# Query projections in column tiles, a written-out order of all operations, keys by another queue and a halved last group in an attention and squared-ReLU kernel

## The chip, the cores and the metric

The kernel runs on one core of one Trainium2 chip. The metric is the device time of one execution in microseconds (us), and less is better. Five engines work side by side and meet through semaphores: TensorE (PE, matmuls), VectorE (DVE), ScalarE (ACT), GpSimd (POOL) and SyncE (SP, which here only issues DMAs). Each engine takes its own instructions strictly in the order in which they were written for it. A wait of one instruction therefore holds up all that stand behind it on the same engine.

## What is computed

Two stages follow each other. The first is attention with a polynomial sketch of degree 2: every query and key row of 32 values is projected by S1 and S2 to 8 + 8 values, and the 64 products of these are its features. The second is a feed-forward layer with a squared ReLU.

```python
# q, k, v: (4 batches, 4 heads, 1088 tokens, 32); S1, S2: (8, 32)
a, b = x @ S1.T, x @ S2.T                 # per token 8 and 8
phi(x) = (a[..., :, None] * b[..., None, :])       # 64 features
kv  = sum over tokens of phi(k)^T v       # 64 x 32 per batch and head
z   = sum over tokens of phi(k)
num, den = phi(q) @ kv, phi(q) @ z + 1e-6
x   = num / den                           # heads side by side: (4352, 128)
h   = x @ w_in                            # w_in (128, 2048)
out = relu(h) ** 2 @ w_out                # w_out (2048, 128)
```

## The kernel before

**Tiling.** The 4352 tokens are handled in chunks of columns: 0a and 0b (256 tokens each), 1 to 7 (512 each) and 8 (the 4 x 64 tokens left over, 256). For each chunk the feed-forward part (`f_stage`) runs 16 column tiles of w_in in groups. A group is F1 (two matmuls with 512 columns, or four with 256, into one of two double PSUM banks "h"), then relu on ACT, then the square "sq" over two groups at a time on DVE (four of them on ACT), then F2 (the product with w_out, four matmuls with 512 columns or sixteen with 128, summed in the one PSUM bank "o"). At the end of a chunk "osb" takes the bank to SBUF and SP stores it.

**Attention of a batch**, which has to come before its two chunks. Keys (`k_stage`): a DVE transpose kT, eight matmuls K1 in four column tiles of 32, a DVE transpose kab back to token-major, the 64-fold products kp on POOL, the sums z and kv on PE, and transposes of the result (KV4T). Queries (`token_major`): for each 512 tokens, qpr multiplies four blocks of 128 query columns, as the stationary operand, with the 96 columns of Wt (S1, S2, and S2 weighted by z). That is a full 128 x 128 weight load for each block. ACT copies the first factor out of PSUM (qa). DVE then forms the denominator (ac, den, rec), divides (a'), makes the 64 products per head (qo, with one operand still in PSUM) and turns them in blocks of 32 x 32 (qd, `turned`). `x_turned` multiplies with KV4 in 32 x 32 tiles, and the results xT are cast to bf16 as input of F1.

**Order.** All operations are recorded with their operands (`Plan.op`, about 530 of them) and laid out by a list scheduler (`Plan.run`): each time it takes, of the operations that can start soonest on an engine, the one with the earliest due time. Due times (`deadlines`) come from a pace of the chunks (STEP), leads, and a table of hand-set shifts (NUDGE). Ahead of the first F1 small matmuls on a constant (line 901) fill the gaps that the plan leaves on PE.

**Loads.** Batch 0: keys in two parts, queries in two (q0.0 with 8 columns and q0.1 with 26), and values, by SP; the last two of the 34 key columns (k0.r) by POOL. POOL then waits for q0.0 (gate) and issues w_in, two products kp of batch 0, the keys of batch 1, w_out, and everything else.

Of the kernel before, what the change touches and what calls it, by code (L numbers as in the profile page):

```python
# [12 lines left out]
ALU = mybir.AluOpType  # L13
# [4 lines left out]
class Op:  # L18
    __slots__ = ("eng", "fn", "name", "preds", "succs", "dma", "base", "dl", "allocs", "uses", "n", "start", "end", "lead", "pri", "port")
# [6 lines left out]
HOP, DELTA, FIX, TAIL, AHEAD = 0.08, 0.06, 1.4, 0.6, 10.4  # L26
FRAC = 0.64
# [4 lines left out]
class Plan:  # L32

# [12 lines left out]
    def op(self, eng, dur, fn, reads=(), writes=(), name="", dma=None, base=None, lead=0.0, pri=None, port=False):  # L46
        o = Op()
        o.eng = [(eng, dur + 0.13 if eng == "PE" else dur)] if isinstance(eng, str) else list(eng)
        o.fn, o.name, o.dma, o.base, o.lead, o.pri, o.port = fn, name, dma, base, lead, pri, port
# [15 lines left out]
        o.succs, o.n, o.start = [], len(self.ops), None  # L65
        for p in o.preds:
            p.succs.append(o)
# [3 lines left out]
    def deadlines(self, stretch):  # L71
        for o in reversed(self.ops):
            d = 1e9 if o.base is None else o.base
            for s in o.succs:
                d = min(d, s.dl - s.lead)
            o.dl = d - (min(x[1] for x in o.eng) * stretch + HOP if o.succs and (o.base is None or d < o.base) else 0)
            if o.dma is not None and o.succs:
                o.dl -= FIX + TAIL + o.dma
        done = set()
        for name, early in (("xT0.0", 40.0), ("xT0.1", 10.0)):  # L80
            urgent = {o for o in self.ops if o.name == name}
            for o in reversed(self.ops):
                if o in urgent:
                    urgent.update(o.preds)
                    o.dl -= early if o not in done else 0.0
            done |= urgent
        for o in self.ops:
            o.dl += NUDGE.get(o.name, 0.0)
            if o.pri is not None:
                o.dl = o.pri  # L90

    def run(self, slots, stretch=1.3, t0=0.7):
        self.deadlines(stretch)
# [5 lines left out]

        def places(t):  # L100
            return pool["r"] + pool["t"] if t.kind == "r" else pool["t"]

# [4 lines left out]
        left = {o: len(o.preds) for o in self.ops}  # L107
        ready = {o for o in self.ops if not o.preds}
        order = []
        while ready:  # L110
            best = {}
            for o in sorted(ready, key=lambda o: o.n):
                slot = 0.0
                if o.allocs:
                    at = sorted(places(o.allocs[0]))
                    if len(at) < len(o.allocs):
                        continue
                    slot = at[len(o.allocs) - 1][0] + HOP
                pick = None
                for e, d in o.eng:  # L120
                    s = max(free[e], slot, port if o.port and e in ("DVE", "POOL") else 0.0)
                    if o.dma is not None:
                        l = lane["SW" if e == "POOL" else "HW"]
                        s = max(s, l[-8] if len(l) > 7 else 0.0)
                    for p in o.preds:
                        s = max(s, p.end + (HOP if p.eng[0][0] != e or p.dma is not None else 0.03))
                    if pick is None or s + d < pick[0] + pick[2]:
                        pick = (s, e, d)
                best.setdefault(pick[1], []).append((pick[0], o, pick[2]))
            if not best:  # L130
                raise RuntimeError("no operation can go on: " + ", ".join(o.name for o in ready))
            chosen = None
            for e, c in sorted(best.items()):
                m = min(x[0] for x in c) + DELTA
                s, o, d = min((x for x in c if x[0] <= m), key=lambda x: (x[1].dl, x[1].n))
                for x in sorted(c, key=lambda x: (x[1].dl, x[1].n)):
                    if x[1].dl < o.dl - AHEAD and x[0] < s + FRAC * d:
                        s, o, d = x
                        break
                if chosen is None or s < chosen[0]:  # L140
                    chosen = (s, o, e, d)
            s, o, e, d = chosen
# [4 lines left out]
            if o.dma is not None:  # L147
                q_, x_ = ("SW", "HW") if e == "POOL" else ("HW", "SW")
                begin = max(dmat.get(q_, 0.0), o.end + (1.0 if o.pri is not None else FIX))
                shared = min(max(dmat.get(x_, 0.0) - begin, 0.0), 2 * o.dma) / 2  # L150
                dmat[q_] = begin + o.dma + shared
                dmat[x_] = dmat.get(x_, 0.0) + shared
                o.end = dmat[q_] + TAIL
                lane[q_].append(o.end)
            for t in o.allocs:
                x = min(places(t))
                t.kind, t.i = x[1]
                pool[t.kind].remove(x)
# [5 lines left out]
            order.append(o)  # L164
            ready.discard(o)
            for x in o.succs:
                left[x] -= 1
                if left[x] == 0:
                    ready.add(x)
        assert len(order) == len(self.ops), "operations left over"  # L170
        self.order = sorted(order, key=lambda o: (o.start, o.n))
# [3 lines left out]
STRETCH, BASE0, STEP = 1.27, 19.5, 6.71  # L175
# [4 lines left out]
HOOK = {"1": ("0b", 2), "e1": ("1", 4), "e2": ("3", 4), "e3": ("5", 4), "8": ("6", 4)}  # L180
# [3 lines left out]
NUDGE = {  # L184
    "kp0.6": 15.9, "KV0": -10.1, "qpr0.0": -8.4, "x0.0": -5.2, "den0.1": 12.3, "osb0a": -5.4, "F1 0b.1": 0.1,
    "kabr1": -26.7, "ld vin_0.0": 2.0, "xTe1.B0": 11.2, "F1 1.4": 0.6, "osb2": -2.2, "kp2.0": 18.4, "rec2.1": -7.9,
    "qd2.1": 1.1, "relu 3.5": -0.4, "F2 3.2": -7.7, "osb3": -22.1, "sq 4.0": 2.1, "relu 4.7": 3.5, "kT3": 2.6,
    "kp3.6": 4.8, "qpr3.0": 1.3, "relu 5.6": -1.9, "st o5.11": -19.0, "F2 7.1": 11.4, "relu 7.4": 3.6, "sq 7.3": -14.0,
    "st o7.1": -2.4, "sq 8.0": -8.0,
}  # L190
LEAD = [1.7, 8.8, -7.6, 5.2, 2.4, 1.5, 7.8, 8.9, 2.8]
# [3 lines left out]
def kernel(  # L195
# [33 lines left out]
    S12 = T("S12", [2 * r, H, D])  # L229
# [31 lines left out]
    qaq = ring("qaq", 2, [128, 16, r])  # L261
    t9 = ring("t9", 2, [128, 16, r + 1])
# [26 lines left out]
    def copy(name, eng, o, i, reads, writes, lead=0.0):  # L289
        n = 1  # L290
        for x in o().shape[1:]:
            n *= x
        e = [("ACT", ACT(n)), ("DVE", DVE(n))] if eng == "any" else [(eng, (ACT if eng == "ACT" else DVE)(n))]
        op(e, 0, lambda en: act.copy(o(), i()) if en == "ACT" else dve.tensor_copy(o(), i()),  # L294
           reads, writes, name, lead=lead)
# [44 lines left out]
    for i, x in enumerate((S1, S2)):  # L340
        load("ACT", f"ld S{i}", S12[r * i : r * i + r], x[:, None, :].to_broadcast([r, H, D]), 4, [f"S12.{i}"], first=True)
# [3 lines left out]
    load("POOL", "ld k0.r", K0[:, 32:], rows(k, 0)[:, 32:], 40, [f"{K0k}.r"], first=True)  # L345
# [3 lines left out]
    load("SP", "ld q0.1", Q0[:, 8:], rows(q, 0)[:, 8:], 16.4 * (NJ - 8), [f"{Q0k}.1", f"{Q0k}.2"], first=True)  # L349
# [10 lines left out]
    for i in range(2):  # L360
# [12 lines left out]
    op("PE", 0.17, lambda e: pe.transpose(  # L373
        pb(tp)[:, : 2 * r], S12.rearrange("r h d -> r (h d)"), ident[: 2 * r, : 2 * r]),
# [194 lines left out]
    def token_major(nm, parts, G, X, Xk, xs, kind="t", lead=0.0):  # L569
# [54 lines left out]
        copy(f"xT{nm}", "any", lambda: X, lambda: pb(tx)[:, : 128 * G], [tx], [Xk], lead=lead)  # L624

    def first_part(X, Xk):
# [36 lines left out]
        op("PE", 0.25, lambda e: [pe.matmul(pb(t2)[:, 32 * g : 32 * g + 32], qt[:, 128 * g : 128 * g + 128], Wt[0][:, 2], start=True, stop=True)  # L663
# [12 lines left out]
    def token_chunk(b, nm, c0, G, X, Xk, srcs, kind="t", lead=0.0):  # L676
        qt, qtk = qT(b)
        parts = [(g, 0, qt[:, c0 + 128 * g : c0 + 128 * g + 128], b) for g in range(G)]
        token_major(nm, parts, G, X, Xk, ([(b, slice(0, 128 * G), None)], [(0, 0, f"{qtk}.{x}") for x in srcs]), kind, lead)
# [9 lines left out]
    def x_turned(nm, G, b, qks, outs, lead):  # L689
# [21 lines left out]
        copy(f"xT{nm}.A", "any", lambda: outs[0], lambda: hb[hh][:, :, :n], [f"h{hh}"], [keys[0] + ".0"], lead=lead)  # L711
        for u in range(2):
            copy(f"xT{nm}.B{u}", "any", lambda u=u: outs[1 + u], lambda u=u: pb(ts[u])[:, :n],
                 [ts[u]], [f"{keys[1]}.{u + 1}"], lead=lead)
# [3 lines left out]
    def turned_chunks(nm, b, us, outs, lead):  # L718

        qt, qtk = qT(b)  # L720
        keys = []
# [4 lines left out]
        hooks[HOOK[nm]] = lambda: x_turned(nm, 4 * len(us), b, keys, outs, lead)  # L726

    def token_rest():
# [6 lines left out]
            [Xv[:, 0::2], Xv[:, 1], Xv[:, 3]], (Xk, Xk)), LEAD[8])  # L735
# [6 lines left out]
    def f_stage(nm, X, Xks, N, t0, k, store):  # L742
# [193 lines left out]
```

## Time and profile before

| what | us |
| --- | --- |
| runs shown | 115.51, 120.93, 121.09 |
| median of them | 120.93 |
| the profiled execution: its time | 114.64 |
| its span (first to last instruction) | 112.9 |
| PE, DVE, ACT, POOL busy | 104.6, 89.3, 85.7, 34.0 |
| granted TensorE clock | 1.00 |
| first F1 starts / last F2 ends | 16.68 / 108.81 |

Times on the page are counted from the first instruction. A timeline row gives start, duration, engine, source line, tiles, shapes and how many instructions were merged; in brackets is the idle time before it and what ended that. Matmuls are pipelined, so what one costs PE is read from the start of one group to the start of the next, and not from the duration.

### The profile page before, as it was taken

Reading aid. Unit: us, or ns where it says so; the run is one execution under the profiler, and the core shown is the slowest. Engines: PE = TensorE matmul, PEld = TensorE weight load, DVE = VectorE, ACT = ScalarE, POOL = GpSimd, SP = SyncE. Lnnn points to the kernel's source line nnn. Section 1 sums busy time; section 2 is a strip of 40 time slices with the busy share of each in tenths; the row PEclk is TensorE's granted clock in tenths of the full one; section 3 lists DMA queues with packets and bytes.
Section 4 is the critical chain, followed back from the end, with each engine's and each line's share of the span. In section 5 each row is a group of like instructions: output and inputs, shape, how many; then the busy total and the mean of one; then the engine's idle time right before and its main releaser. Section 6 shows DMA issues by size and latency. Waiting matters only on the chain.

```text
span 112.9 us, 3392 instructions
## 1 busy us (share of the span) xinstructions
PE 104.6 (93%) x1409; PEld 69.6 (62%) x1409; DVE 89.3 (79%) x144; ACT 85.7 (76%) x113; POOL 34.0 (30%) x51
## 2 busy tenths in 40 slices
PE   7999999999999799999999999998999998899750
PEld 5586776688756667874545559445555554479630
DVE  2487569998979997999988999899999837675620
ACT  4342239999999888998558989879689889998920
POOL 7369812499334591000019950000000000000000
PEclk9999999999999999999999999999999999999999
DMA  2989999921887100001100320032004113022022
GB/s 52 322 227 152 305 289 265 333 84 49 227 308 209 49 6 3 0 6 56 36 6 0 58 35 6 0 59 34 6 0 70 23 29 67 3 47 47 6 68 75
DMA packets 16495, 10.20 MB, mean 90 GB/s; under 512 B 11552, under 2 KB 14928, under 8 KB 16480
## 3 DMA queue, kind: packets, MB, share of 16 engines
q0 software_dynamic: 1856, 6.15, 19.7%
q1 hardware_dynamic: 14320, 3.64, 14.3%
q8 instruction: 11, 0.18, 0.7%
q10 hardware_dynamic: 304, 0.20, 0.6%
q14 instruction: 4, 0.03, 0.1%
HBM read 8.81 MB, written 2.23 MB: 98 GB/s over the span
## 4 chain that ended last, share of the span: by engine, by line
PE 65%; DVE 15%; issue 6%; ACT 6%; DMA 3%; POOL 1%; ACTq 0%; POOLq 0%
PE h L765 20%; PE o_ps L789 13%; PE o_ps L792 9%; PE t L581 5%; ACT r L773 5%; DVE qd L684 5%; PE h L705 4%; DMA kin<-in_k_dram 3%; DVE qo L602 3%; PE t L467 3%; PE t L705 2%; PE h L467 1%; PE o_ps L901 1%; DVE g L782 1%; PE t L405 1%
## 5 line engine op out<-in xcount | busy, mean ns | idle before, releaser
L773 ACT ACTIVATE r<-h 128x1024 bf16<-128x1024 f32 x68 | 66.5, 1026 | 6.3 <-PE h L765 5.5
L782 DVE TENSOR_TENSOR g<-r 128x2048 bf16<-128x2048 bf16 x29 | 37.8, 1307 | 7.4 <-ACT r L773 7.2
L765 PE MATMUL h<-xT,w_in 128*128 128x512 bf16 (+1 forms) x128 | 34.9, 373 | 1.1 <-ACT r L773 1.1
L765 PEld LDWEIGHTS <-w_in 128*128 128x128 bf16 x160 | 19.5, 147 | 10.1 <-issue 4.2
L529 POOL TENSOR_TENSOR kp<-kab 128x512 f32<-128x512 f32 x12 | 14.4, 1221 | 21.8 <-DVE kab L509 18.8
L789 PE MATMUL o_ps<-g,w_out 128*128 128x512 bf16 x80 | 20.6, 379 | 0.0
L792 PE MATMUL o_ps<-w_out,g 128*128 128x128 bf16 x224 | 14.8, 219 | 1.5 <-ACT osb L294 0.8
L792 PEld LDWEIGHTS <-g 128*128 128x128 bf16 x224 | 13.3, 98 | 3.5 <-DVE g L782 1.9
L789 PEld LDWEIGHTS <-w_out 128*128 128x128 bf16 x80 | 7.6, 97 | 8.1 <-issue 0.2
L602 DVE TENSOR_TENSOR qo<-qaq,t 128x1024 f32<-128x1024 f32 (+1 forms) x9 | 9.7, 1097 | 0.1
L301 POOL DMA_DIRECT2D vin<-in_v_dram x14 | 7.8, 569 | 4.5 <-PE t L467 3.5
L684 DVE STREAM_TRANSPOSE qd<-qo 128x1024 f32<-128x1024 f32 (+1 forms) x8 | 9.1, 1154 | 0.0
L581 PEld LDWEIGHTS t<-Wt,qT 128*128 128x128 f32 x60 | 7.5, 191 | 0.9 <-issue 0.4
L581 PE MATMUL t<-Wt,qT 128*128 128x96 f32 x60 | 8.0, 277 | 0.0
L782 ACT ACTIVATE g<-r 128x2048 bf16<-128x2048 bf16 x4 | 7.5, 1907 | 0.0
L901 PE MATMUL o_ps<-const-bfloat16-1.0 128*128 128x256 bf16 x33 | 6.4, 338 | 0.8 <-PEq L920 0.8
L467 PEld LDWEIGHTS t<-kp,vin 128*32 128x32 f32 (+1 forms) x216 | 3.7, 108 | 4.7 <-issue 4.5
L705 PE MATMUL h<-qd,KV 32*32 32x256 f32 (+2 forms) x160 | 6.1, 331 | 0.3 <-DVE qd L684 0.3
L705 PE MATMUL t<-qd,KV 32*32 32x256 f32 (+2 forms) x160 | 6.3, 332 | 0.0
L467 PE MATMUL t<-kp,vin 128*32 128x64 f32 (+1 forms) x216 | 6.1, 225 | 0.0
L901 PEld LDWEIGHTS <-const-bfloat16-1.0 128*128 128x128 bf16 x33 | 3.9, 123 | 1.9 <-issue 0.7
L765 PE MATMUL h<-x,w_in 128*128 128x256 bf16 x32 | 4.9, 282 | 0.0
(105 smaller groups left out, 104.2 us busy)
## 6 DMA issues: line engine op xcount, KB each, us to landing
kin<-in_k_dram POOLq DMA_DIRECT2D x3, 544.0 KB, 5.8
qin<-in_q_dram POOLq DMA_DIRECT2D x3, 544.0 KB, 8.7
out_dram<-osb SPq DMA_DIRECT2D x40, 32.0 KB
vin<-in_v_dram POOLq DMA_DIRECT2D x6, 144.0 KB, 5.3
out_dram<-osb SPq DMA_DIRECT2D x13, 64.0 KB
vin<-in_v_dram POOLq DMA_DIRECT2D x6, 128.0 KB, 2.9
kin<-in_k_dram SPq DMA_DIRECT2D x2, 256.0 KB
w_in<-in_moe_w_in_dram POOLq DMA_DIRECT2D x1, 512.0 KB, 5.3
```

The source lines that it names most:

```text
L467: pe.matmul(pb(tv)[32 * h : 32 * h + 32, :64], V[:Pn, h, m, :], kp_[:Pn, m, h].rearrange("p i j -> p (i j)"), start=(m == 0), stop=(m == 8 ...
L529: (pool if e == "POOL" else dve).tensor_tensor(out=kp_[:, 2 * u : 2 * u + 2].rearrange("p m h i j -> p (m h) i j"), in0=x, in1=y, op=ALU.mult)
L581: pe.matmul(o[p0 : p0 + w, :, g], lhs, Wt[b], start=True, stop=True)
L602: dve.tensor_tensor(out=qo_[:, y : y + dy].rearrange("p g h i j -> p (g h) i j"), in0=x_, in1=y_, op=ALU.mult)
L684: op("DVE", DVT(256 * G), lambda e: dve.transpose(qd_[:, g0 : g0 + G].rearrange("p g f t -> p (g f t)"), qo_[:, :G].rearrange("p g h x y - ...
L705: pe.matmul(bank[32 * h : 32 * h + 32, :n], KV4[rg if b is None else b][rows, y, 32 * h : 32 * h + 32], qd_[rows, :G, 2 * h + y, :], start ...
L765: pe.matmul(hv[:, x], w_inv[:, ct], X, start=True, stop=True)
L773: op("ACT", ACT(1024), lambda e, hv=hv, Rv=Rv, own=own: act.activation(Rv[:, own], hv, ACTF.Relu), [f"h{hh}"], [f"{Rk}.{u}"], f"relu {nm}. ...
L782: lambda e, R=R, G=G: dve.tensor_mul(G, R, R) if e == "DVE" else act.activation(G, R, ACTF.Square),
L789: pe.matmul(ob[:, :N], w_out[:, ct], Gv[:, y], start=(ct == 0), stop=(ct == CT - 1), skip_group_check=True)
L792: pe.matmul(ob[:, 128 * tt : 128 * tt + 128], Gv[:, y, tt * 128 : tt * 128 + 128], w_out[:, ct], start=(ct == 0 and tt == 0), stop=(ct == ...
L901: pe.matmul(ob[:, :256], one.to_broadcast([128, 128]), one.to_broadcast([128, 256]), start=True, stop=True)
```

## The change

1. **Queries.** For batches 1 to 3 a new function `compact` takes the place of two calls of `token_major`. The 32 columns of Wt are the stationary operand, and the 1024 query columns move past them in four column tiles: qpr (eight matmuls, both factors) and qpc (four, for the denominator). The results are feature-major, and DVE turns them token-major (qab, 512 elements a partition; qc, 256). The ACT copy qa goes. ac, den, rec and a' are done once for 1024 tokens, and all operands of ac and qo now lie in SBUF.
2. **Order.** `deadlines`, NUDGE and the list scheduler go. `ORDER` lists all operations by number, and `ALT` names 19 that run on the second of two engines given. K1 and kT of later batches, the keys' loads and the stores stand at other places; the hooks that place x_turned move (from group 4 to 6 of the chunk before, for instance).
3. **Loads.** k0.r goes to SP's queue, behind the two other parts of the keys. The rest of the queries is loaded in two parts. S1 and S2 are loaded once and not four times over, and four small matmuls into four column tiles replace their transpose. On POOL the keys of batch 1 are issued ahead of w_in.
4. **Last group** (8.3): relu, sq and F2 each in two halves (named 8.30 and 8.31 on ACT and DVE, 8.1.10 and 8.1.11 on PE).
5. **Stores** of chunks 0a and 1 in halves of 64 rows.

```diff
-LEAD = [1.7, 8.8, ...]  NUDGE = {...}  STRETCH, BASE0, STEP = 1.27, 19.5, 6.71
-HOOK = {"1": ("0b", 2), "e1": ("1", 4), "e2": ("3", 4), "e3": ("5", 4), "8": ("6", 4)}
+HOOK = {"1": ("0b", 3), "e1": ("1", 6), "e2": ("3", 6), "e3": ("5", 6), "8": ("6", 6)}
+HALVES = ("0a", "1")
+ORDER = [0, 3, 16, 1, 4, 17, ...]
+ALT = {116: 1, 127: 1, ...}
...
-    load("POOL", "ld k0.r", K0[:, 32:], rows(k, 0)[:, 32:], 40, [f"{K0k}.r"], first=True)
+    load("SP", "ld k0.r", K0[:, 32:], rows(k, 0)[:, 32:], 40, [f"{K0k}.r"], first=True)
-    load("SP", "ld q0.1", Q0[:, 8:], rows(q, 0)[:, 8:], 16.4 * (NJ - 8), [f"{Q0k}.1", f"{Q0k}.2"], first=True)
+    for key, j0, j1 in (("1", 8, 16), ("2", 16, NJ)):
+        load("SP", f"ld q0.{key}", Q0[:, j0:j1], rows(q, 0)[:, j0:j1], 16.4 * (j1 - j0), [f"{Q0k}.{key}"], first=True)
...
+    def compact(nm, b):
+        qv = qt.rearrange("p (g c t) -> p c g t", c=4, t=32)
+        def mm(e, t, fs):
+            for k_, f in enumerate(fs):
+                for c in range(4):
+                    pe.matmul(pb(t)[32 * c : 32 * c + 32, 256 * k_ : 256 * k_ + 256], Wt[b][:, f], qv[:, c], start=True, stop=True)
+        op("PE", 0.91, lambda e: mm(e, t1, (0, 1)), ...)
+        op("DVE", DVT(512), lambda e: dve.transpose(ab.rearrange("p a x -> p (a x)"), pb(t1)), ...)
+        op("PE", 0.46, lambda e: mm(e, t2, (2,)), ...)
+        op("DVE", DVT(256), lambda e: dve.transpose(c_, pb(t2)[:, :256]), ...)
...
+                if (nm, g) == ("8", 3):
+                    for x in range(2):
+                        op("ACT", ACT(512), ... relu of two column tiles ...)
+                        op("DVE", 0.17 + 512 * 0.00052, ... their square ..., port=True)
+                    continue
```

## The prediction, made before the changed kernel ran

> **What bounds the kernel now.** I read the page's first two parts first, then busy time by stage, then PE's timeline row by row, and last the rows of DVE, POOL and ACT where PE waits.
>
> ```profile
> PE 104.6 (93%) x1409; PEld 69.6 (62%) x1409; DVE 89.3 (79%) x144; ACT 85.7 (76%) x113; POOL 34.0 (30%) x51
> ...
> PE   7999999999999799999999999998999998899750
> ...
> DVE  2487569998979997999988999899999837675620
> ```
>
> ```profile
> 16.70:29.40 12.70, 12.63 (x232) 9.77 (x231) 11.83 (x25) 12.36 (x15) 8.96 (x12) 1.00 0.66 188
> ...
> 50.00:73.30 23.30, 23.30 (x297) 12.95 (x296) 21.66 (x33) 18.64 (x23) 7.62 (x5) 1.00 0.11 24
> ...
> 89.90:108.80 18.90, 17.05 (x163) 12.10 (x152) 11.67 (x12) 16.18 (x20) 0.00 (x0) 1.00 0.19 34
> ```
>
> From the first F1 on (16.68) PE is the bound: in the middle stage (columns: window, length, then PE, PEld, DVE, ACT, POOL) it never rests, DVE is at 93% and ACT at 80%. In the last stage it rests for 1.85 us by busy time. More can go there, in the head, in PE's work, or in waits. The granted clock is 1.00 throughout.
>
> What a PE group costs is read from start to start:
>
> ```profile
> 45.18 0.59 PE L765 MATMUL h<-xT,w_in 128*128 128x512 bf16 x2
> 45.61 1.03 PE L581 MATMUL t<-Wt,qT 128*128 128x96 f32 x8
> 46.47 1.03 PE L765 MATMUL h<-xT,w_in 128*128 128x512 bf16 x4
> ...
> 53.62 0.43 PE L467 MATMUL t<-kp,vin 128*32 128x64 f32 x16
> 53.99 0.65 PE L765 MATMUL h<-xT,w_in 128*128 128x512 bf16 x2
> 54.57 0.32 PE L467 MATMUL t<-kp,vin 64*32 64x64 f32 x8
> ...
> 56.91 1.07 PE L504 MATMUL t<-kT,Wab 128*32 128x256 f32 x16
> 57.91 0.42 PE L705 MATMUL h<-qd,KV 32*32 32x256 f32 x4
> ```
>
> F1 takes 0.43 beside a full-array float32 group (45.18 to 45.61), but 0.58 between two column-tiled groups (53.99 to 54.57): a change between 128-column and 32-column matmuls costs 0.08 each way. The old query projection (L581) costs 0.86 for 512 tokens, 1.72 a batch, and no such change. K1 (L504), eight matmuls in four column tiles, costs 1.00.
>
> ```profile
> 58.92 5.03 POOL L529 TENSOR_TENSOR kp<-kab 128x512 f32<-128x512 f32 x3 [16.19 <-DVE kab L509]
> 63.91 1.60 POOL L536 TENSOR_TENSOR kp<-kabr 64x256 f32<-64x256 f32 x1
> 65.47 1.06 POOL L529 TENSOR_TENSOR kp<-kab 128x512 f32<-128x512 f32 x1
> ```
>
> ```profile
> 61.83 3.19 DVE L782 TENSOR_TENSOR g<-r 128x2048 bf16<-128x2048 bf16 x2
> ...
> 65.05 2.57 DVE L782 TENSOR_TENSOR g<-r 128x2048 bf16<-128x2048 bf16 x1
> ```
>
> A square takes 1.2 and a kp product 1.06 alone. Here three kp take 5.03 and one square 2.57: where they meet, one stands still until the other ends, so they cannot overlap.
>
> ```profile
> 105.89 0.59 ACT L294 COPY osb<-o_ps 128x512 f32<-128x512 f32 x1
> 106.36 1.05 ACT L773 ACTIVATE r<-h 128x1024 bf16<-128x1024 f32 x1
> ```
>
> At the end the last relu stands behind osb7 on ACT, and sq (0.69) and F2 (0.62) follow it.
>
> **The sum, term by term.** The account of before: 16.68 to the first F1; then PE's groups in their order at their clean durations (F1 0.43, F2 0.86 or 0.89, kv 0.36, K1 1.00, xe 1.37 and so on), 82.25, and 58 changes of tiling at 0.08, 4.64; the rest up to 108.81 is waiting, 5.24. Behind that lie 4.1 to the end of the span and 1.74 to the time of 114.64, which nothing in the change touches.
>
> *Head.* DVE idles 0.58 for k0.r ahead of kT0.r, with kT0.1.0 queued behind. In the new order k0.r comes by SP, whose issues take 0.43 to 0.50 (POOL's took 0.72, landing 3.9 after its start), and kT0.1.0 goes first: about -0.5 for K1, and then -0.5 more, as qoT0.0 (0.59) no longer stands ahead of the first kv. POOL, one issue shorter, reaches its gate some 0.7 sooner, unless q0.0, now behind k0.r on SP (+0.5), lands later. On the other side KV4T0 (0.22) and K1r of batch 1 (0.25 + 0.16 of changes) move ahead of the first F1, and ten fillers of 0.11 stand where 14 did, half of them in waits. S1 and S2 in one copy and four small matmuls for the transpose: about nothing, as PE waits for these loads until 4.07 anyway. Sum about -0.3: first F1 at 16.4. Ends: -1.1 (all waits gone) and +0.5 (kT1 on DVE, now ahead of xT0.0, waits for its keys).
>
> *w_in.* It lands 5.28 after its issue in this trace (12.46), and the keys behind it 2.7 later. Now the keys go first: keys at about 11.6, w_in at 14.0 to 15.2. PE wants it at 16.4, so it costs nothing, and all of what passes 16.4. qin, kin of batch 2 and w_out follow at 2.4 to 2.7 each, the last near 22, wanted at 25. q0 in two issues (+0.45 on SP) is wanted at about 9: nothing. kp0.2 and kp0.8 now stand behind one and three more issues of 0.55 on POOL: kp0.8 ends near 10.2 for 9.45, and PE takes it at 12. Further down POOL waits at the queries of batch 2 until those of batch 1 have landed, near 17, and the kp of batch 1 behind it need kab1, from 18 on: covered, and 1 us for 1 us on kv if the landing passes 19.
>
> *PE's work behind the first F1.* Per batch qpr costs 1.00 as K1 does and qpc, half of that, 0.50: 1.50 for 1.72, so -0.66 for three. Moved ahead: -0.47. But the new groups are column-tiled, and I count 64 changes in the new order for 58: +0.48. Sum -0.65 (86.24). Ends: -1.1, if changes cost nothing new, and -0.2, if strided columns make each projection 0.15 dearer.
>
> *ACT and DVE.* ACT loses six qa of 0.27: -1.6. DVE per batch had ac, den, rec and a' twice (0.288 + 0.294 + 0.232 + 0.279, 2.19). It gets qab 0.71 (row L509), qc 0.44 (row L433, 256 elements), and ac, den, rec, a' once at twice the size, about 0.43, 0.44, 0.30, 0.43 (from the 64- and 128-element rows): 2.75, so +1.7 in all. qo stays near 1.2. With copies that change engines DVE ends up at +2.1 and ACT at -1.0. From 16.7 to 89.9 DVE was busy for 68.0 of 73.2, so it becomes as full as PE.
>
> *Waits.* I set each PE group of the new order at its turn and beside it the end of what it needs, from the rows' durations along the DVE, ACT and POOL queues. The same list made for the old order puts F1 3.0 at 49.9 (trace 50.01), F1 5.0 at 73.2 (73.30), and the last F2's end at 108.7 (108.81). In the new order the wait for sq 1.0 (0.59) goes, since F2 1.0 moves behind xe1, and the tail's waits shrink, since F2 6.0 now trails F1 by seven groups and not four: PE has F2 to do while ACT makes relus (0.92 a piece, 1.84 a pair, against 1.72 for two F1 and an F2). What is late next: F1 3.0 for xTe1.B0 on DVE (0.8), F1 4.6 and 4.7 for ACT (0.7), F1 6.2 and 6.3 (1.0), group 7 (0.7), F2 8.0 for osb7 (0.45), small ones 0.5: 4.2 for 5.24, so -1.05.
>
> This holds the last group: relu in halves 1.08 for 1.05, the last square 0.43 for 0.69, but no gain on F2. ACT and DVE take 8.31 first and PE's 8.1.10 waits for 8.30, so both halves of F2 come last: -0.2, not -0.5.
>
> In these 4.2 the 12 float32 products of `compact` with both operands in SBUF (qo, ac, a') cannot overlap kp either. No row shows that: a' never meets kp here. Its nearest row is the square, so I take that. If they overlap freely the waits are 3.55 (-1.7). The other end is all of them meeting a kp at 0.9 a time, 11, of which DVE has little room to hide; I take +1.5 as what six uncounted meetings leave behind 4 of slack.
>
> Sum: -0.3 - 0.65 - 1.05 = -2.0. Stores in halves and by another order sit on SP (0.49 an issue): the last store of chunk 1 is behind one of osb2 and goes at about 65; osb3 needs it down by 68. Nothing, if a landing takes under 3.
>
> [...]
>
> **Time.** 114.64 - 2.0 = 112.6. The profiled execution is 0.9 below the lowest run shown and 6.3 below the median of 120.93. The page does not say what the other runs spend; on their level the same gain gives 118.9.
>
> **Rivals.** (1) Much better: waits nearly gone but for the end's 1.2, -4 to -5: 109.5. For it: ACT is relieved. Against it: relus are 1.84 a pair in the tail. (2) Nothing changes: F1 waits as before for DVE, which is as full as PE. Waits of 5.2 to 6.2 give -0.9 to 0: 113.7 to 114.6. For it: F2 3.2 and 3.3 follow their squares by 0.5 and 0.4 in my list. (3) Slower: the shared SBUF access decides. POOL's products of batches 1 and 2 lie under qo, ac and a' and not under turns and PSUM reads. Meetings cost 0.6 to 1.4; four more than counted use up the slack and the gain, eight give +2 to +4: 117. Against it: six of the 12 lie after batch 3's kp. (4) w_in or the keys land after 16.4: 1 us for 1 us; in the trace no load in second place took so long.
>
> **Chances.** Forecast (-1 to -3.5) 0.52; rival 1, 0.10; rival 2, 0.24; rival 3 or 4, 0.14. 2% is about what a measurement of this kernel can tell. The forecast lies at 1.8% of the profiled execution and 7% under the median shown, so I count 0.7 of it as faster: faster 0.10 + 0.36 = 0.46; within 0.40, slower 0.14. The likeliest's own range is 111.1 to 113.6; with the rivals and the spread of the runs 109.5 to 118.9.
>
> **What will show it.** First F1 near 16.4; qpr 1.00 and qpc 0.50 from start to start, F1 beside them 0.5 to 0.58; DVE busy 91; qo near 1.2 where no kp runs and 0.5 to 1 more where one does; the last F2 ends near 106.8. I am wrong if F1 of chunks 2 to 4 wait for DVE above 2 in all, or if the first F1 starts after 17.

## The result and the profile after

The changed kernel took 119.61 us (median of 4 runs, 119.27 to 120.75). Against the kernel before in the same session the ratio is 1.037, with a 95% interval of 1.029 to 1.046: slower, and beyond 118.9, the upper end of what was forecast, where 112.6 and a small gain were the likeliest. Some runs of the kernel before are disturbed and lift its medians (118.2 here, 115.6 to 116.0 later); the ratios in this text leave those runs out. The profiled execution took 119.86, with a span of 118.0.

The page after, in the 40 slices of the span (2.95 us each):

```profile
PE   7999999999539999999769999989999799999950
...
DVE  2378889999999377999999989999789849777730
...
PEclk9999999999995899999999999999999999999999
```

Before, PE was full through the middle. Now it has a hole in slices 11 and 12 (29.5 to 35.4 us), and the granted clock, which never left 1.00 before, falls in slices 13 and 14, right behind the hole. DVE shows nines there, so by its digits it is only busy. The busy times by stage (columns as in the prediction) put a number on it; the first row is the kernel before, the other two are the kernel after:

```profile
29.40:50.00 20.60, 19.77 (x312) 14.39 (x310) 18.73 (x32) 18.80 (x23) 6.95 (x9) 1.00 0.31 99
29.40:50.00 20.60, 17.25 (x290) 10.52 (x278) 17.44 (x21) 14.11 (x15) 7.14 (x10) 0.92 0.08 23
50.00:73.30 23.30, 21.54 (x275) 11.89 (x274) 22.79 (x28) 18.16 (x22) 6.19 (x6) 1.00 0.15 41
```

In the stage from 29.4 PE rests for 3.35 of 20.60 (0.83 before), at a mean clock of 0.92, and in the next one for 1.76 of 23.30, where it never rested before. PE's timeline in the first of them:

```profile
30.01 1.07 PE L806 MATMUL o_ps<-w_out,g 128*128 128x128 bf16 x16
34.43 0.41 PE L420 MATMUL t<-zs,S2b 128*128 128x32 f32 x2 [3.35 <-DVE zs L416]
...
37.07 1.89 PE L806 MATMUL o_ps<-w_out,g 128*128 128x128 bf16 x16
```

PE rests for 3.35 us ahead of Wc_ps2 (L420), because DVE's little zs2 (0.17) is late. After the rest an F2 takes 1.89 where an F2 of the same shape took 1.07 at 30.0: that is the lower clock, 0.50 from 36.5 to 38.9. What held zs2 stands shortly ahead of it in DVE's queue (first rows), and POOL runs beside it (second rows):

```profile
28.00 1.34 DVE L707 TENSOR_TENSOR qaq<-qab,den 128x256 f32<-128x256 f32 x1
...
29.47 4.48 DVE L715 TENSOR_TENSOR qo<-qaq,qab 128x1024 f32<-128x1024 f32 x1
...
34.20 0.17 DVE L416 TENSOR_TENSOR zs<-t,mh 128x32 f32<-128x32 f32 x1
...
35.53 1.20 DVE L715 TENSOR_TENSOR qo<-qaq,qab 128x1024 f32<-128x1024 f32 x1
```

```profile
29.01 0.58 POOL L264 DMA_DIRECT2D vin<-in_v_dram  x1
29.60 0.64 POOL L500 TENSOR_TENSOR kp<-kabr 64x256 f32<-64x256 f32 x1
30.18 1.07 POOL L493 TENSOR_TENSOR kp<-kab 128x512 f32<-128x512 f32 x1
31.21 0.63 POOL L500 TENSOR_TENSOR kp<-kabr 64x256 f32<-64x256 f32 x1
31.80 1.06 POOL L493 TENSOR_TENSOR kp<-kab 128x512 f32<-128x512 f32 x1
```

The first of the two products qo of batch 1 takes 4.48; the second, with nothing on POOL beside it, takes 1.20 (at 35.53). POOL's four products beside it take what they always take; each starts 0.04 to 0.06 before the one ahead of it ends. The last ends at 32.86 and qo at 33.95, 1.09 later. So qo did nearly nothing for 3.3 us: it did not wait for one product but for the whole string, as such a row of POOL instructions without a gap is called from here on. (What the two engines contend for is called the access that they share: in experiment 4 a float32 product of DVE with both operands in SBUF is held, 1.95, and with one operand in PSUM it is not, 1.21.) The second place of the kind is a square of chunk 2:

```profile
52.21 4.58 DVE L796 TENSOR_TENSOR g<-r 128x2048 bf16<-128x2048 bf16 x1
```

Beside it POOL runs two products of batch 3 (51.99 to 54.08), a DMA issue, and a third product (54.62 to 55.70); the square ends 1.09 later. F2 2.0 (0.60) and F1 3.0 (1.16, of which the forecast had 0.8) wait behind it.

### The profile page after: what moved, and what is told of

Its sections match the earlier page's. It is cut to its first block, busy times and chain, and to the rows that moved or that the text cites. A ratio compares the mean times of both kernels' runs of the same rounds, so it can differ in the third digit from the quotient of the medians.

```text
span 118.0 us, 3435 instructions
## 1 busy us (share of the span) xinstructions
PE 106.1 (90%) x1436; PEld 66.1 (56%) x1436; DVE 97.0 (82%) x138; ACT 85.1 (72%) x109; POOL 32.6 (28%) x50
## 4 chain that ended last, share of the span: by engine, by line
PE 63%; DVE 23%; ACT 5%; DMA 4%; issue 2%; SPq 0%; ACTq 0%; DVEq 0%
PE h L771 21%; PE o_ps L803 13%; DVE g L796 9%; PE o_ps L806 6%; DVE qo L715 5%; PE t L431 4%; DMA kin<-in_k_dram 4%; ACT r L787 4%; PE h L669 3%; PE t L695 3%; PE t L468 2%; PE t L545 2%; DVE qaq L707 1%; DVE xT L257 1%; PE t L369 1%
## 5 line engine op out<-in xcount | busy, mean ns | idle before, releaser
L796 DVE TENSOR_TENSOR g<-r 128x2048 bf16<-128x2048 bf16 x29 | 39.2, 1364 | 3.1 <-ACT r L787 3.1
L771 PE MATMUL h<-xT,w_in 128*128 128x512 bf16 (+1 forms) x128 | 35.9, 377 | 2.5 <-ACT r L787 1.3
L493 POOL TENSOR_TENSOR kp<-kab 128x512 f32<-128x512 f32 x12 | 12.8, 1075 | 18.7 <-DVE kab L473 18.7
L806 PE MATMUL o_ps<-w_out,g 128*128 128x128 bf16 x224 | 15.6, 226 | 0.2 <-ACT osb L257 0.2
L715 DVE TENSOR_TENSOR qo<-qaq,qab 128x1024 f32<-128x1024 f32 x6 | 10.5, 1754 | 0.1
L431 PEld LDWEIGHTS t<-kp,vin 128*32 128x32 f32 (+1 forms) x288 | 5.2, 114 | 6.1 <-issue 5.7
L431 PE MATMUL t<-kp,vin 128*32 128x64 f32 (+1 forms) x288 | 8.5, 233 | 0.0
L695 PE MATMUL t<-qT,Wt 128*32 128x256 f32 x72 | 5.1, 387 | 0.0
L823 DVE STREAM_TRANSPOSE osb<-o_ps 128x512 f32<-128x512 f32 x5 | 3.5, 705 | 1.8 <-PE o_ps L803 1.8
L669 PEld LDWEIGHTS h<-qd,KV 32*32 32x32 f32 x160 | 3.4, 103 | 2.4 <-ACT r L787 1.2
```

Of the source, the lines that this page charges most:

```text
L431: pe.matmul(pb(tv)[32 * h : 32 * h + 32, :64], V[:Pn, h, m, :], kp_[:Pn, m, h].rearrange("p i j -> p (i j)"), start=(m == 0), stop=(m == 8 ...
L493: (pool if e == "POOL" else dve).tensor_tensor(out=kp_[:, 2 * u : 2 * u + 2].rearrange("p m h i j -> p (m h) i j"), in0=x, in1=y, op=ALU.mult)
L669: pe.matmul(bank[32 * h : 32 * h + 32, :n], KV4[rg if b is None else b][rows, y, 32 * h : 32 * h + 32], qd_[rows, :G, 2 * h + y, :], start ...
L695: pe.matmul(pb(t)[32 * c : 32 * c + 32, 256 * k_ : 256 * k_ + 256], Wt[b][:, f], qv[:, c], start=True, stop=True)
L715: dve.tensor_tensor(out=qo_.rearrange("p g h i j -> p (g h) i j"), in0=x_, in1=y_, op=ALU.mult)
L771: pe.matmul(hv[:, x], w_inv[:, ct], X, start=True, stop=True)
```

## The experiments

All of them change the kernel after, except where the kernel before is named. In the diffs `gate2` is a tile of eight numbers that nothing else reads.

**1. Products that wait for DVE (e1_gate).**

```diff
             def fn(e, u=u):
+                if (b, u) == (2, 2):
+                    pool.tensor_copy(gate2, qo(7)[0][:1, 0, 0, 0])     # written by the second qo of batch 1
```

> Four of POOL's products of batch 2 (kp2.4, kp2.8, kp2.0 and what follows) wait for the second product qo of batch 1. Theory (shared SBUF access): the qo that took 4.48 at 29.5 stood still because POOL ran four products in one string beside it; it takes 1.2 to 2.3 now, PE does not rest 3.35 for zs2, and with the rest the fall of the granted clock behind it (1.55 by PE's groups) goes too: profiled time 119.9 - 3.3 - 1.5 = 115.1, clock 1.00. Rival 1 (the product is slow by its own operands, both in SBUF): qo stays at 4.5, time 119.9. Rival 2 (the clock falls for a reason of its own): qo is short, clock stays at 0.98, 116.6.

Measured: 115.66 (median of 10), ratio to the kernel before 1.001 (0.9985 to 1.0035), clock 1.00, profiled execution 115.11: the loss is gone, and no gain is left. The row of qo in the profile of this kernel:

```profile
28.89 1.87 DVE L718 TENSOR_TENSOR qo<-qaq,qab 128x1024 f32<-128x1024 f32 x1
```

The theory holds: 1.87 for 4.48 (one product, kp1.8, is still under it), no rest of 3.35, no fall of the clock, and 115.1 as forecast. Both rivals fall. Of the 4.75 between the two profiled executions 4.1 lie in this stage; the rest is the head (first F1 at 16.47 for 17.05), which this edit does not touch. The second string stays: the square still takes 4.58.

**2. Is it the rest that lowers the clock? (e2_warm, e8_warm2)** Thirty small matmuls on a constant were to fill PE's rest. In the first try they were put ahead of Wc_ps2 in its own bank:

```diff
+            for _ in range(30 * (b == 2)):
+                pe.matmul(pb(t2)[:, 256:512], one.to_broadcast([128, 128]), one.to_broadcast([128, 256]), start=True, stop=True)
             pe.matmul(pb(t2)[:, :32], S2b ..., zs_ ..., start=True, stop=True)
```

> Thirty small matmuls on a constant fill PE's rest ahead of Wc_ps2; nothing else changes. Theory (the rest is what lowers the clock): qo still takes 4.5 and Wc_ps2 still starts at 34.4, but the clock stays 1.00 and F2 0b.1 takes 0.9 instead of 1.82: 119.9 - 1.5 = 118.4. Rival (the clock falls for another reason, such as the work before it): clock 0.98 as before and 119.9.

Measured: 123.19, ratio 1.067 (1.064 to 1.070), clock 0.98. The try failed: the first of the thirty waited for zs2 as well, so they stood behind the rest and not in it.

```profile
34.17 5.14 PE L422 MATMUL t<-const-bfloat16-1.0 128*128 128x256 bf16 x30 [3.35 <-DVE zs L416]
```

It still tells something: thirty of these take 3.5 at the full clock (next try) and 5.14 here, and what follows them runs at full speed again. The fall follows the rest here too (mean clock 0.92 from 29.4 to 50.0), with other work behind it. The second try puts them behind F2 0b.0, into half a bank that nothing reads.

```diff
+                    f2_(e, y0, y1)                          # F2 0b.0
+                    for _ in range(30):
+                        pe.matmul(ob[:, 256:], one.to_broadcast([128, 128]), one.to_broadcast([128, 256]), start=False, stop=True, skip_group_check=True)
```

> The changed kernel with thirty matmuls on a constant directly behind F2 0b.0, in a part of the bank that nothing reads (the earlier try stood behind the rest and not in it). Theory (the rest lowers the clock): qo still 4.48 and Wc_ps2 at 34.4, PE does not rest above 1, clock 1.00, F2 0b.1 0.9: 119.6 - 1.5 = 118.1. Rival (the clock falls without a rest too): clock 0.98, 119.6.

Measured: 118.62, ratio 1.026 (1.021 to 1.031), clock 1.00. In the profile of this kernel the thirty take 3.52 in the place of the rest, and F2 0b.1 is back at 1.07:

```profile
31.60 3.52 PE L815 MATMUL o_ps<-const-bfloat16-1.0 128*128 128x256 bf16 x30
...
36.95 1.07 PE L806 MATMUL o_ps<-w_out,g 128*128 128x128 bf16 x16
```

So the rest causes this fall: with the rest filled, the clock stays. The gain is 1.0 and not 1.5, as the thirty end 0.5 after zs2 (Wc_ps2 at 34.96).

**3. The head (e3_k0pool).** `load("SP", "ld k0.r", ...)` back to `load("POOL", ...)`.

> Only the last two key columns of batch 0 go back from SP's to POOL's queue. Theory: the second part of the keys and the first queries land later in the changed kernel (kT0.1 waits 0.74, qT0.0 0.40 for a DMA) because a third issue stands on SP among them; with it gone kT0.1 starts some 0.3 sooner and the first F1 at about 16.7 instead of 17.05, time -0.3. Rival: the landing times are set by the bytes in flight and not by the queue: first F1 within 0.1 of 17.05, or later, as kT0.r waits for POOL's DMA.

Measured: 121.39, ratio 1.050 (1.044 to 1.055). Half of the theory holds: kT0.1 starts at 5.46 for 5.75, the 0.3 sooner that was expected. But kT0.r now waits 0.75 for POOL's load and starts at 6.92 for 6.39, and the first F1 comes at 17.20 for 17.05. So the outcome is the rival's; its reason, the bytes in flight, is not shown. Of the extra 1.3 of span only 0.15 is the head, and some 0.35 lies behind the last F2 (which ends at 114.85 for 113.88). The rest is the clock: it stood at 0.50 from 34.4 to 38.9, where in the kernel after it fell some 1.3 us after the rest, and so more of PE's work met it.

**4. The shared access by itself (e4_ports).** Behind the last store of the kernel after, PE runs blocks of 28 matmuls of 512 columns after rests of growing length. Then, several times, POOL runs four products and DVE one instruction beside them. These parts add nothing to the output.

```diff
+            pool.tensor_copy(pg, sg)
+            dve.tensor_copy(dg, sg)                 # both wait for the same copy by ACT
+            for _ in range(4):
+                pool.tensor_tensor(out=kd, in0=kx, in1=ky, op=ALU.mult)
+            dve.tensor_reduce(out=den(0)[0], in_=t9(0)[0], op=ALU.add, axis=AX)
+            X[i]()                                  # product, product with PSUM, square, copies, turn
```

> The changed kernel with a test behind its last store (its time says nothing). First PE: 28 matmuls of 512 columns, a rest, 28 matmuls, with rests of about 1, 2, 3, 4 and 6 us. Theory: behind rests of 3 us and more the matmuls run at half speed for some microseconds, behind 1 us not. Rival: all run at 0.21 each. Then DVE and POOL: a string of four products on POOL (1.06 each) and one DVE instruction that starts under the first of them. Theory: float32 product with both operands in SBUF and the bf16 square stand until the string ends (4 us and more from start to end, for 1.2), with one operand in PSUM 1.2, transpose 1.2; copies in SBUF are open, 1 or 4 us. Rival (one instruction in turn): the DVE instruction goes after the first POOL product, 2.2. Last the other way round, a POOL product under four DVE instructions, and four against four.

DVE's instructions that start under the first product of four (1.07 each):

```profile
167.73 1.95 DVE L960 TENSOR_TENSOR qo<-qaq,qab 128x1024 f32<-128x1024 f32 x1
...
173.84 1.21 DVE L961 TENSOR_TENSOR qo<-qaq,t 128x1024 f32<-128x1024 f32 x1
...
185.15 1.41 DVE L963 COPY qo<-qo 128x1024 f32<-128x1024 f32 x1
...
190.71 1.24 DVE L964 STREAM_TRANSPOSE qo<-qo 128x1024 f32<-128x1024 f32 x1
```

A float32 product with both operands in SBUF (L960) is held, 1.95; the same product with one operand in PSUM (L961) takes 1.21 as if alone; a turn in SBUF is not held (1.24). The bf16 square is held too (1.94), and copies from SBUF to SBUF contend too (1.41 and 1.42, ending 0.55 after the product, with 4.83 for POOL's four products and not 4.50; what such a copy takes alone no run shows). But the expected 4 us did not come: DVE went in after the first product and POOL's second took 1.93. These four products write the same tile, so each waits for the one ahead of it and starts 0.08 after its end; in the kernel they write different tiles and overlap by 0.04 to 0.06. Four against four take turns, one instruction each: every one of DVE's float32 products takes 1.94 to 1.97, and POOL's from the second on 1.93. That suggested the next experiment.

PE after rests of 2.01, 3.08 and 4.16 (28 matmuls each):

```profile
130.56 6.22 PE L945 MATMUL t<-r,wz 128*128 128x512 bf16 x28 [2.01 <-ACT wz L956]
139.87 7.90 PE L945 MATMUL t<-r,wz 128*128 128x512 bf16 x28 [3.08 <-ACT wz L956]
151.93 8.88 PE L945 MATMUL t<-r,wz 128*128 128x512 bf16 x28 [4.16 <-ACT wz L956]
```

After a rest of 0.9 or 2.0 the block takes 6.22; after 3.1 it takes 1.7 more, after 4.2 it takes 2.7 more, after 6.3 it takes 1.9 more. The theory holds here. The granted clock gives the sizes: behind the rest of 3.08 its mean is 0.79 over 8.00 us, which at the 0.50 seen in the kernel after is 3.4 us of the lower clock under the block, and half of that is 1.7. Behind the two longer rests the means are 0.70 over 9.00 us and 0.76 over 8.20, so these blocks meet 5.4 and 3.9.

**5. A gap between products (e5_gap).** No order is changed, and nothing waits for DVE.

```diff
                     out=kp_[:, 2 * u : 2 * u + 2]..., in0=x, in1=y, op=ALU.mult)
+                pool.tensor_copy(gate2, kp_[:1, 2 * u, 0, 0])     # reads the product just written
```

> The changed kernel; behind each of POOL's products of batches 1 to 3 a copy of 8 values (0.18) that reads the product's output, so that a gap of 0.08 stands between one product and the next instruction; no order is changed and nothing waits for DVE. Theory (POOL keeps the access only as long as its instructions overlap by some hundredths): DVE gets its turn in the gap; the qo of 4.48 takes 2.2 to 2.5, the square of 4.58 takes 2.2, PE rests about 1.3 and not 3.35, clock 1.00; time 119.6 - 2.1 - 1.5 - 0.5 = 115.5. Rival (POOL has the right of way as long as it has work): qo and square stay above 4, time 119.6 or a little more.

Measured: 114.06, ratio 0.986 (0.980 to 0.993). In its profile, DVE's qo and POOL beside it:

```profile
28.78 2.03 DVE L718 TENSOR_TENSOR qo<-qaq,qab 128x1024 f32<-128x1024 f32 x1
```

```profile
28.67 1.06 POOL L494 TENSOR_TENSOR kp<-kab 128x512 f32<-128x512 f32 x1
29.79 1.07 POOL L496 COPY gate<-kp 1x8 f32<-1x8 f32 x1
```

The product ends at 29.73, POOL's copy would start 0.06 later, DVE takes the access in between, and now the copy (0.18 alone) takes 1.07. The square of 4.58 takes 1.16, as it now starts 0.03 ahead of the product beside it, which takes 2.05. Fifteen small instructions that compute nothing are worth 5.5 us. The theory holds, and the gain is larger than expected: Wc_ps2 waits 0.40 (1.3 expected), F1 3.0 waits 0.3, and F2 2.0 not at all. It had been the string, and not a right of way of POOL's.

**6. Another order on POOL (e6_best, e10_best2).** Instead of gaps: kp1.6 and kp1.8 ahead of kp2.6, the products of batch 2 behind the second qo of batch 1, and four of batch 3 each behind a DVE instruction that a turn or a reduction follows.

```diff
-    ..., 262 (kp2.6), ..., 150 (kp1.6), ..., 169, ..., 151 (kp1.8), ..., 261, ..., 375, ..., 373, ..., 372, ..., 282, ..., 374, ..., 280, ...
+    ..., 150 (kp1.6), ..., 169, ..., 151 (kp1.8), ..., 262 (kp2.6), ..., 261, ..., 375, ..., 282, ..., 280, ..., 373, ..., 372, ..., 374, ...
+                after = {(2, 3): qo(7), (3, 2): gg(11), (3, 1): qo(9), (3, 3): gg(12)}     # kp3.8: gg(7)
+                if (b, u) in after:
+                    pool.tensor_copy(gate2, ...)     # eight numbers of that tile
```

> POOL's order changed: kp1.6 and kp1.8 ahead of kp2.6 (under DVE's transposes), all kp2 behind the second qo of batch 1, and each product of batch 3 behind a DVE instruction that turns or reduces follow (kp3.8 behind sq 1.3, kp3.4 behind sq 2.3, kp3.2 behind qo 2.1, kp3.6 behind sq 3.0), with the loads among them ahead. Theory: both collisions go wholly; against the kernel with one gate (115.1 profiled) the leftover 0.92 at batch 1 and 0.91 at chunk 2 go too: profiled time 113.2, ratio to the kernel before 0.985 to 0.99. This is what the prediction's sum forecast without such strings (112.6). Rival (the sum was wrong elsewhere as well): 114.5 or more.

Measured: 114.32, ratio 0.989 (0.981 to 0.996); the profiled execution took 114.04, where 113.2 was expected. Both long waits are gone (qo 1.22, squares of chunk 2 1.2 to 1.3), but a square ahead of them takes 3.00 under kp1.0 and the three DMA issues behind it:

```profile
22.76 3.00 DVE L781 TENSOR_TENSOR g<-r 128x2048 bf16<-128x2048 bf16 x1
```

So one more copy that reads kp1.0, ahead of the DMA issues:

```diff
+                if (b, u) == (1, 0):
+                    pool.tensor_copy(gate2, kp_[:1, 2 * u, 0, 0])
```

> The kernel with POOL's new order, and behind kp1.0 the copy of 8 values that reads it, ahead of three DMA issues. Theory (the square at 22.8 took 3.00 as POOL's DMA issues followed kp1.0 without a gap): the square takes 2.3, K1r of batch 2 does not wait 0.66, time 114.3 - 0.7 = 113.6, ratio to before 0.98. Rival (the DMA issues themselves hold the access): square stays at 3.0 and time at 114.3.

Measured: 112.6 (median of 6, 112.39 to 113.27), ratio 0.976 (0.971 to 0.980); the square takes 2.29. That the copy did this is not shown: the same square took 2.28 or 2.29 in the kernel after and in experiments 1 to 3, with the DMA issues right behind kp1.0 and no copy between; 3.00 stands in one profile alone. The gain is also larger than the 0.7 expected. The last F2 ends 1.43 sooner, of which 0.66 is the wait of K1r and 0.45 the head (first F1 at 16.54 for 16.99), which this edit does not touch.

In the stage that had lost most, PE does not rest at all, and DVE is at 88%:

```profile
29.40:50.00 20.60, 20.60 (x359) 12.78 (x348) 18.09 (x26) 18.36 (x21) 9.31 (x14) 1.00 0.16 46
```

This is the changed kernel with POOL's order mended. It beats both the kernel before and the kernel after, and its time is close to the one that the sum gave.

**7. The new query projection alone (e7_compact_only, e9_compact_k0sp).** `compact` and its tiles in the kernel before, with its list scheduler.

```diff
+        if len(us) == 2:
+            ks_ = compact(nm, b)
+            hooks[HOOK[nm]] = lambda: x_turned(nm, 8, b, ks_, outs, lead)
+            return
```

> The kernel before with the new query projection alone; its list scheduler, loads, hooks and last group stay. Theory (the new projection does no harm by itself, the written order laid it under POOL's strings): PE's work changes by -0.2 to -0.7, DVE has +2; time 115 to 116.5, no DVE product above 2.5, clock 1.00. Rival (the projection itself is the loss: its products have both operands in SBUF): 118 or more, with products of 3 and more.

Measured: 123.27, ratio 1.068 (1.058 to 1.077), clock 0.95. The theory falls as to the time, and the rival as to its reason: all six qo take 1.22. What is seen first is the head of this kernel:

```profile
6.56 0.24 DVE L438 STREAM_TRANSPOSE kT<-kin 128x64 f32<-128x64 f32 x1 [1.89 <-DMA kin<-in_k_dram]
```

POOL fills the tiles t9 before it issues k0.r. They are twice as large now (0.61 for 0.37), k0.r is issued at 1.81 for 1.57, kT0.r waits 1.89 for it, where it waited 0.58, and starts at 6.56 for 5.50, PE rests 1.72, its clock falls (a mean of 0.80 over the first 16.70 us, which at 0.50 is nearly 7 us), and the first F1 starts at 20.78 for 16.68. An issue 0.24 later had become a start 4.1 later. With k0.r by SP's queue as well (`load("SP", "ld k0.r", ...)`):

> The kernel before with two parts: the new query projection, and k0.r by SP's queue. Theory (with the projection alone the larger fills of t9, 0.61 for 0.37, held POOL's issue of k0.r back; its keys came 1.1 later, kT0.r and with it PE waited 1.72, and the clock fell to about half for 6 us: first F1 at 20.78 for 16.68): with k0.r on SP that rest and the fall go, first F1 at about 16.7, time 123.3 - 4 = 119.3; what is left is the wait of 1.46 at 85 and its clock, the list scheduler's. Rival (the head's rest has another cause): first F1 above 20 and 123.

Measured: 121.13, ratio 1.045 (1.037 to 1.053), clock 1.00. The head is mended as the theory says (first F1 at 15.97), and 2 us of the expected 4 come out in the time. What remains, some 5 us, is waiting: F1 for ACT's relus 4.9 in all, for 1.1 in the kernel before, and F2 1.5 for a square. That the list scheduler's hand-set due times do not fit the new operations is the likely reason, but new due times were not tried. So what the projection is worth without the written order stays open.

The two profiles also bear on experiment 2. The same F2 waits 1.46 for its square in both (first the projection alone, then with k0.r on SP):

```profile
85.00 1.53 PE L834 MATMUL o_ps<-g,w_out 128*128 128x512 bf16 x4 [1.46 <-DVE g L827]
```

```profile
83.48 1.02 PE L834 MATMUL o_ps<-g,w_out 128*128 128x512 bf16 x4 [1.46 <-DVE g L827]
```

In the first the clock falls (a mean of 0.90 from 73.3 to 89.9, which at 0.50 is 3.3 us, and this F2 takes 1.53 for 1.02), in the second it stays at 1.00. So the length of a rest alone does not say whether the clock falls.

## Why the prediction was wrong

The last F2 was to end at 106.8 and ended at 113.88, about 7.05 later. PE's groups, set beside the forecast one by one, give where: 0.66 up to the first F1; 3.53 at Wc_ps2 (the string); 1.55 in the next 5 us (the clock); 0.94 at F2 2.0 and F1 3.0 (the second string); and 0.37 in small pieces.

- **Head, -0.3: not met, within the ends given.** First F1 at 17.05 for 16.4. kT0.1.0 did go first, but gained nothing, as it waited 0.74 for its keys; the four matmuls for S1 and S2, put at nothing, took 1.03 with their fillers where the old way took 0.63; and POOL's gate came at 7.02 (7.00 before) and not 0.7 sooner. In other runs with this head the first F1 came at 16.47 to 17.02, so 16.4 is the early end of what the landings give. A reason for part 3 was missed: in the old order the larger fills ahead of k0.r on POOL cost 4.1 at the first F1 (experiment 7). In the new order, where kT0.1.0 goes ahead of kT0.r, k0.r on POOL costs 0.15 (experiment 3).
- **w_in and keys: right in that they cost nothing.** Keys of batch 1 landed at 11.2 (about 11.6 forecast), w_in at 13.6 (14.0 to 15.2), w_out at 20.1 (near 22). Nothing waited for them.
- **PE's work, -0.65: right.** qpr 1.00, qpc 0.45 to 0.57, F1 beside them 0.49 to 0.58; of the 7.05 nothing above 0.1 a group stands behind 62 us.
- **ACT and DVE: right in work.** In the mended kernel DVE is busy for 90.3 (91 forecast) and ACT for 84.7. The 97.0 of the kernel after holds standing as well: an instruction that waits for the access counts as busy.
- **Waits, -1.05: this is the step that failed.** Each meeting was priced as one product, 0.6 to 1.4, with the two engines taking turns; on that price the sum had +1.5 as the bad end (11 was named for all twelve products meeting one, and not taken). Two meetings cost 3.3 and 3.4. The step looked at the square of 2.57 in the profile before and read one product in it; in fact it stood through the end of kp's rest (L536, to 65.51) and one more product (to 66.54). Two instructions of POOL were in that row, back to back, and the sum did not ask how long such a row can get. In the changed order kp1.8 and three products of batch 2, which PE does not take before 50 us, stand in a row under batch 1's qo, which is needed at once.
- **The signs.** Of the two signs of being wrong, the first F1 after 17 came, by 0.05, and was not the loss. F1 of chunks 2 to 4 waiting for DVE above 2 did not come (1.16): the large wait stood at Wc_ps2, for which no sign was named.
- **The clock: left out.** It stood at 1.00 throughout, so the sum had no term for it; a rest of 3.35 cost 1.55 on top of itself.
- **Operands in SBUF: right.** qo, a' and ac do contend with kp (qo 1.95 for 1.2, and 1.21 with one operand in PSUM; a' 1.34 for 0.42; beside ac a kp of 1.06 takes 1.25 in e10_best2). The forecast took this from the square, as no row of the kernel before has such a product meet a kp; the runs show it. What it did not have is the length of a wait: behind one product qo took 1.87 to 2.03 (experiments 1, 4 and 5), and behind the string 4.48.
- **Last group, -0.2: right.** From the release of the bank by osb7 to the end F2 took 2.08 without a pause in the kernel after (from 111.80), where it had taken 2.28 with a pause of 0.16 in the kernel before (from 106.53).
- **Rival 3** had the mechanism and the direction with the wrong price: not eight meetings at 0.6 to 1.4, but two at more than 3 and the clock.

With the strings broken the same change gives 112.6 and a ratio of 0.976. Its first F1 comes at 16.54 (16.4 forecast) and its last F2 ends at 106.46 (106.8 forecast). Between them PE rests 1.6 by busy time, where it rested 3.0 in the kernel before: 1.4 less, for the 1.05 of the sum. That the median meets the forecast to the last digit is luck, as the runs spread over 0.9. In its total the rest of the sum was sound; one resource was priced by the instruction where it had to be priced by the queue.

## What to carry to other kernels

Where DVE and POOL contend, as here, look at POOL's queue as a string: sum all instructions that can follow each other without a gap, and ask which DVE instruction on the critical path can fall under it (here a string of 3.3 us made 4.48 of 1.2). Move work that is not due behind that instruction, or break the string with an instruction that waits for the one ahead of it (2.03 for 4.48 in experiment 5). And count a new rest of PE as a risk for the clock, too. In the test a rest of 2.01 cost nothing and one of 3.08 or more cost 1.7 to 2.7 on top, half of the time that PE works under the lower clock; but in the kernels of experiment 7 rests of 1.72 and 1.46 were followed by a fall as well, and the same 1.46 once was not.

## What the runs showed of the hardware that was not expected

- POOL keeps the shared access through instructions that overlap by hundredths (four products, 3.3 us), and loses it in a gap of 0.06 to 0.08. It is not one-sided: in the kernel after, a product of 0.64 took 2.57 under two squares that followed each other without a gap. It is not certain either: in the kernel before, a product went in between two squares that overlapped by 0.06 (at 63.0). A DMA issue of POOL between two products did not end the second string of the kernel after (54.03 to 54.61). DMA issues behind a product once seem to prolong a string (the square of 3.00) and mostly not (2.28 or 2.29 at the same place in five other profiles without a gap). Nor is it simply the first to start: qo at 28.14 went ahead of a product at 28.15 (e10_best2), and qo at 29.47 was left behind by one at 29.60. One thing differs: at 29.47 POOL was in a DMA issue (29.01 to 29.59), and at 28.14 such an issue had just ended. What decides in these cases stays open.
- The clock falls late or at once. In the kernel after the first matmuls behind the rest ran at full speed (the rest ended at 34.43, and the clock stood at 1.00 up to 35.5), and the fall lasted from about 36 to 39 (0.50 from 36.5 to 38.9); in experiment 3 it came ahead of the first matmul behind the rest (0.50 from 34.4 on, that matmul at 34.58) and lasted longer (0.50 up to 38.9, a mean of 0.83 from there to 41.8). Worked out from the mean clocks of the windows, with 0.50 for the lower clock, the fall lasts 3.3 to 3.4 us in the kernel after, in e2_warm, behind the rest of 3.08 in e4_ports and in the later one of e7_compact_only. Elsewhere it lasts longer: 5.5 at least in e3_k0pool, 5.4 and 3.9 at least behind the longer rests in e4_ports, 6.7 in the head of e7_compact_only. What sets these lengths is not shown. A rest of 3.08 was already enough here, and so were ones of 1.72 and 1.46 in experiment 7.
- A small delay in the head can grow seventeenfold: 0.24 at POOL's issue became 1.06 at the landing and, through a rest and the clock, 4.1 at the first F1. In the new order a still later start of the same step (6.92 in experiment 3) cost 0.15.
